# Nineteen joined score activations instead of thirteen, and one group of query transposes a place later, in a softcap attention with a soft mixture of experts on one core

## The chip, the cores and the metric

The kernel runs on one core of a Trainium2 chip. The metric is the device time of one execution in microseconds. The kernel before takes 281.36 us (median of three runs, 280.99 to 281.57).

Engine names are those of the profile: PE is TensorE (PEld its weight loads), ACT is ScalarE, DVE is VectorE, POOL is GpSimd, SP is SyncE. A line such as L366 is line 366 of the kernel.

## What is computed

Attention with a soft cap over 8 batches, 12 heads, 448 positions and 64 columns a head, then a soft mixture of eight experts over the 3584 rows of 768 columns that the attention leaves:

```python
scores = scale * np.matmul(q, k.transpose(0, 1, 3, 2))
scores = cap * np.tanh(scores / cap)
attn = np.exp(scores - max)                 # then divided by its sum
x = attn @ v                                # -> 3584 x 768
logits = x @ phi                            # 768 -> 32 slots
d = softmax(logits, over all rows)
slot_input = d.T @ x                        # 32 slots, 4 an expert
slot_out[e] = relu(slot_input[e] @ w1[e]) @ w2[e]
out = softmax(logits, over the slots) @ slot_out
```

## The kernel before, in words

**Tiles and steps.** Four heads of one batch are a *quad* (24 quads, three a batch); a quad has two pairs of heads, and a pair has seven *tiles*, each of 64 keys of both its heads against their 448 queries. That makes 336 tiles. `turn` puts them into one fixed order in which the second pair of a quad is interleaved with the first pair of the next one. The main loop (`for j in range(NCH)`) has 56 *steps* of six tiles. A step j has two *halves* of three tiles, i = 2j and 2j + 1.

**One step.** `qk_chunk(i)` computes the scores of a half: six matmuls on PE (L349) into three PSUM banks, a bank a tile. `tanh_chunk(i)` is the tanh on ACT, from PSUM to SBUF (L366, 128 x 1344 elements). `exp_chunk(j)` is the exponential on ACT, in SBUF (L374). Of most steps one, two or three of the six tiles are left out of it (`SHARED`), and DVE computes their exponential in seven instructions (`poly_exp`, L602 to L609), whose places in the loop are written out by hand in `POLY`. `pv_first`, `pv_tail` and `pv_rest` multiply the exponentials of a pair with its values on PE (L627), and `norm` ends the pair on DVE with a reciprocal (L634) and a multiplication (L637).

**Joined steps.** In the steps listed in `JOINED` one ACTIVATE (L362, 128 x 2688) does the tanh of both halves. From the first joined step to the last one the six score banks are one tile, the *board*, whose two halves are released separately; outside that stretch they are two tiles of three banks that take turns. In a joined step both halves come free together, at the end of that one ACTIVATE.

**The order of the work** is the order of the program: each engine takes its instructions in the order in which the loop emits them. A step has the slots 0, m, e, a, b, r, c and d, and each of them but r has a part ahead (`<`) and a part behind (`>`). In a step j: slot 0; the tanh of half 2j; slot m; the tanh of half 2j + 1 (in a joined step, here the one of both); slot e; the exponential of step j - 1; `pv_first`; slot a; `pv_tail`; `qk_chunk(2j + 2)` if the step isn't joined; slot b; `pv_rest` and `norm` (slot r between `norm`'s two instructions); `qk_chunk(2j + 2)` if the step is joined; slot c; `qk_chunk(2j + 3)`; slot d.

**The transposes.** `transp` turns the queries or the keys of a quad: 14 transposes on PE (L279) into one PSUM buffer (tag T, a single buffer, which the other transposes use too) and a copy on DVE to `qT` or `kT` (L281). `WHEN` gives the slots, counted from the batch's first step 7b. `k1` and `q1` are the keys and queries of quad 3b + 1; of batch 0 they have places of their own. From batch 1 on, `k1` stands in slot m and `q1` in slot b of step 7b. By the order of tiles, the first tile of quad 3b + 1 is the third tile of half 14b + 3, for every b from 1 to 7: that is `qk_chunk(2j + 3)` of the very same step j = 7b. Quads 3b + 1 have the numbers 4, 7, 10, 13, 16, 19 and 22; the steps 7b are 7, 14, 21, 28, 35, 42 and 49.

After the loop (L1053 and behind) come the end of the last batch, the two layers of the experts and the output.

Of the kernel before, what the change touches and what calls it, by code (L numbers as in the profile page):

```python
# [37 lines left out]
def kernel(  # L38
# [272 lines left out]
    def half_of(i):  # L311

        nonlocal psS
        j, half = divmod(i, CH // CS)
        if JOINED and half == 0 and j in (JOINED[0], JOINED[-1] + 1):
            scp.close()
            psS = scp.enter_context(tc.tile_pool(name=f"psS{j}", bufs=2 - (j == JOINED[0]), space=PSUM,
                                                 reuse_waits="tile"))
            if j == JOINED[0]:
                own["board"] = psS.tile([P, CH, 512], F32, name="sc", tag="board")  # L320
        if JOINED and JOINED[0] <= j <= JOINED[-1]:
            return own["board"][:, half * CS:half * CS + CS, :]
        return psS.tile([P, CS, 512], F32, name="sc", tag="sc")

    def in_board(j):
        return JOINED and JOINED[0] <= j <= JOINED[-1]

# [27 lines left out]
    def tanh_chunk(i):  # L355
# [3 lines left out]
        sc = scores.pop(i)  # L359
        if j in JOINED:  # L360
            if half:
# [16 lines left out]

    JOINED = (10, 14, 17, 21, 24, 28, 29, 31, 35, 38, 42, 45, 49)
    SHARED = {1: (2, 0), 3: (3, 0), 4: (3, 0), 6: (2, 0), 7: (3, 0), 9: (3, 0), 11: (3, 0), 12: (3, 0), 14: (3, 0), 16: (3, 0), 18: (3, 0), 19: (3, 0), 21: (3, 0), 23: (3, 0), 25: (3, 0), 26: (3, 0), 28: (3, 0), 30: (3, 0), 32: (3, 0), 33: (3, 0), 35: (3, 0), 37: (3, 0), 39: (3, 0), 40: (3, 0), 42: (3, 0), 44: (3, 0), 46: (3, 0), 47: (2, 0), 48: (2, 0), 49: (3, 0), 51: (2, 0), 52: (1, 0), 53: (3, 0), 54: (1, 0)}
    POLY = {(1, 'm'): ((1, 0),),
            (1, 'e'): ((1, 1),),
# [416 lines left out]
    def quad_in(Q, cast_k, cast_q, k_in, q_in, v_in):  # L801
        if 0 < Q < NQ:
# [5 lines left out]
                for n in range(2):  # L808
                    at(*v_in, vcast, Q, n)

    WHEN = {'k1': (0, 'm'), 'q1': (0, 'b'), 'v1': (3, 'c'), 'k2': (2, 'a'), 'q2': (2, 'd'), 'v2': (7, 'b'),
# [4 lines left out]
    for b in range(B):  # L816
        j, p = b * PER, 6 * b

        def when(nm):
            return j + WHEN[nm][0], WHEN[nm][1]  # L820

# [352 lines left out]
    for n in range(B // 2 * NT):  # L1174
        bb, c = divmod(n, NT)
# [59 lines left out]
```

## Time and profile before

| what | value |
|---|---|
| time, median of three runs | 281.36 us (280.99 to 281.57) |
| span of the profiled execution, first to last instruction | 279.2 us |
| PE matmul, busy | 247.0 us (88%) |
| ACT, busy | 248.6 us (89%) |
| DVE, busy | 239.1 us (86%) |
| POOL, busy | 142.0 us (51%) |
| granted clock of PE, mean | 0.985 |
| main loop, by ACT's rows | about 6 to 235 us |

The profiled execution's time is known from its span alone; the difference of 2.2 us to the median of the runs lies ahead of its first and behind its last instruction, or between executions. A row of the timeline reads: start in us from the span's start, length in us, engine, line, operation, what it writes <- what it reads, shape, count of instructions that the row merges, and in brackets the idle time of the engine before it with what ended it.

### The profile page before, as it was taken

To read this page: it belongs to the slowest core of one execution; us is meant where nothing else is said; L and a number is where in the kernel's file an instruction comes from. 1 tells how busy PE (TensorE), PEld (TensorE's weight loads), DVE (VectorE), ACT (ScalarE), POOL (GpSimd) and SP (SyncE) were. 2 spreads that over 40 slices of the span, in tenths; PEclk is the share of its full clock that TensorE was granted. 3 is DMA by queue.
4 is the path that set the end of the run, shared out by engine and by line. 5 is a ranking of instruction groups with operands and counts; after the bars stand their busy time and mean duration, and the time that the engine had idled before them with its cause. 6 is when DMAs were issued, how large, how long until landed. Compare 5 with 4: busy or idle time off the path is not lost.

```text
span 279.2 us, 10421 instructions
## 1 busy us (share of the span) xinstructions
PE 247.0 (88%) x4560; PEld 166.6 (60%) x4560; DVE 239.1 (86%) x473; ACT 248.6 (89%) x195; POOL 142.0 (51%) x198
## 2 busy tenths in 40 slices
PE   8898989998999999989999999899999999998720
PEld 7555556756675766566756675657566678553300
DVE  3479999999999999999999999999999997347940
ACT  4999999999999999999999999999999998237720
POOL 8796548662957296728673758375743230200000
PEclk9999999999999999999999999999999999999995
DMA  6999999999999999999999999999999588979997
GB/s 197 277 193 202 219 219 234 229 221 219 224 225 220 219 229 226 225 217 229 223 226 212 213 219 231 218 210 215 231 217 215 117 279 293 367 290 383 434 424 312
DMA packets 57340, 68.08 MB, mean 244 GB/s; under 512 B 4048, under 2 KB 53840, under 8 KB 56784
## 3 DMA queue, kind: packets, MB, share of 16 engines
q0 software_dynamic: 42448, 35.31, 80.0%
q1 hardware_dynamic: 14704, 32.02, 32.6%
q8 instruction: 35, 0.57, 0.7%
q10 hardware_dynamic: 144, 0.10, 0.1%
q14 instruction: 9, 0.07, 0.1%
HBM read 91.72 MB, written 19.27 MB: 398 GB/s over the span
## 4 chain that ended last, share of the span: by engine, by line
ACT 38%; DVE 27%; PE 27%; issue 3%; POOL 1%; ACTq 0%; DVEq 0%
ACT ex L366 15%; ACT ex L374 15%; PE pv L627 8%; ACT ex L362 6%; DVE xq L637 4%; PE sc L349 3%; DVE xp L605 3%; DVE xp L607 3%; DVE ex L608 2%; DVE ex L602 2%; PE so_ps L1098 2%; PE hp L1070 2%; DVE xf L604 2%; DVE ex L609 2%; DVE xp L606 2%
## 5 line engine op out<-in xcount | busy, mean ns | idle before, releaser
L366 ACT ACTIVATE ex<-sc 128x1344 f16<-128x1344 f32 (+1 forms) x87 | 112.9, 1402 | 0.9 <-PE sc L349 0.9
L374 ACT ACTIVATE ex<-ex 128x1344 bf16<-128x1344 f16 (+5 forms) x58 | 110.7, 1916 | 0.1
L627 PE MATMUL pv<-vbd,ex 128*128 128x130 bf16 (+1 forms) x1610 | 94.0, 212 | 7.6 <-POOL vbd L289 3.4
L627 PEld LDWEIGHTS <-ex 128*128 128x128 bf16 (+1 forms) x1680 | 75.6, 101 | 34.9 <-issue 6.2
L289 POOL CAST vbd<-vraw 64x896 bf16<-64x896 f32 x46 | 47.3, 1028 | 57.3 <-PE pv L627 35.7
L349 PE MATMUL sc<-qT,kT 64*64 64x448 bf16 x672 | 66.0, 359 | 6.7 <-ACT ex L366 4.8
L362 ACT ACTIVATE ex<-sc 128x2688 f16<-128x2688 f32 x13 | 33.6, 2586 | 0.0
L349 PEld LDWEIGHTS <-kT 64*64 64x64 bf16 x672 | 22.1, 105 | 16.3 <-ACT ex L366 6.9
L637 DVE TENSOR_TENSOR xq<-pv,rec 128x448 bf16<-128x448 f32 x46 | 28.7, 625 | 1.6
L607 DVE TENSOR_TENSOR xp<-xp,xf 128x1344 f16<-128x1344 f16 (+2 forms) x34 | 27.1, 798 | 0.6
L608 DVE TENSOR_TENSOR ex<-ex,xp 128x1344 uint16<-128x1344 uint16 (+2 forms) x34 | 26.9, 791 | 0.2
L605 DVE TENSOR_TENSOR xp<-xf 128x1344 f16<-128x1344 uint16 (+2 forms) x34 | 26.8, 789 | 0.2
L116 POOL DMA_DIRECT2D w1b<-in_moe_w_dram x32 | 26.3, 825 | 0.0
L602 DVE TENSOR_SCALAR ex<-ex 128x1344 uint16<-128x1344 f16 (+2 forms) x34 | 17.0, 500 | 1.4 <-ACT ex L366 0.8
L606 DVE TENSOR_SCALAR xp<-xp 128x1344 f16<-128x1344 f16 (+2 forms) x34 | 17.2, 505 | 0.6
L281 DVE COPY kT<-kps 128x896 bf16<-128x896 bf16 x23 | 14.2, 617 | 4.0 <-PE kps L276 2.8
L297 POOL MEMSET vbd<- 64x1 bf16 x22 | 2.8, 129 | 28.6 <-PE pv L627 28.3
L604 DVE TENSOR_SCALAR xf<-ex 128x1344 uint16<-128x1344 uint16 (+2 forms) x34 | 16.7, 491 | 0.4
L185 POOL DMA_DIRECT2D qb<-in_q_dram x22 | 16.3, 740 | 1.2 <-PE qps L279 0.5
L609 DVE TENSOR_SCALAR ex<-ex 128x1344 uint16<-128x1344 uint16 (+2 forms) x34 | 16.4, 483 | 0.4
L120 POOL DMA_DIRECT2D w2d<-in_moe_w_dram x21 | 16.4, 816 | 0.0
L185 POOL DMA_DIRECT2D kb<-in_k_dram x22 | 16.3, 739 | 0.0
(124 smaller groups left out, 320.2 us busy)
## 6 DMA issues: line engine op xcount, KB each, us to landing
w1b<-in_moe_w_dram POOLq DMA_DIRECT2D x32, 384.0 KB, 10.2
vraw<-in_v_dram SPq DMA_DIRECT2D x44, 224.0 KB, 6.2
w2d<-in_moe_w_dram POOLq DMA_DIRECT2D x21, 384.0 KB, 9.9
w2t<-w2d SPq DMA_DIRECT2D x21, 384.0 KB, 6.2
qb<-in_q_dram POOLq DMA_DIRECT2D x22, 224.0 KB, 8.2
kb<-in_k_dram POOLq DMA_DIRECT2D x22, 224.0 KB, 8.1
w2b<-in_moe_w_dram POOLq DMA_DIRECT2D x11, 384.0 KB, 9.5
out_dram<-ob SPq DMA_DIRECT2D x2, 1536.0 KB, 7.7
```

What stands on the lines that cost most here:

```text
L116: pool.dma_start(out=w1b[e][:, js, fs], in_=w1r[:, e, js, fs])
L185: pool.dma_start(out=t, in_=quad_ap(nm, Q))
L289: pool.tensor_copy(vbds[Q % 2][r, :, :, c0:c0 + DH], raw[r])
L349: ins = pe.matmul(sc[cs, u, 0:S], qkT["k", Q][r, c, cs], qkT["q", Q][r, :, cs], start=True, stop=True).ins
L362: apart["t", i - 1] = apart["t", i] = act.activation(exs[j].bitcast(F16), own["board"][:, :, 0:S], ACT.Tanh, scale=qk_scale / cap).ins
L366: ins = act.activation(exs[j][:, half * CS + u0:half * CS + u1, :].bitcast(F16), (own[0] if i == u0 == 0 else sc)[:, u0:u1, 0:S], ACT.Tanh ...
L374: act.activation(exs[j][:, u0:u1, :], exs[j][:, u0:u1, :].bitcast(F16), ACT.Exp, scale=cap)
L605: lambda: dve.tensor_tensor(p, s, s.bitcast(F16), op=ALU.mult),
L607: lambda: dve.tensor_tensor(p, p, s, op=ALU.mult),
L608: lambda: dve.tensor_tensor(y, y, p, op=ALU.add),
L627: pe.matmul(out_, exs[j][r, u, q0:q0 + (HP if tail else P)], v_, start=(c == 0 and g == gs[0] < NF), stop=(c == NT - 1), skip_group_check= ...
L637: dve.tensor_tensor(xq[Q][:, h, s0:s1, :], pv[:, 0:s1 - s0, 0:DH], rec.to_broadcast([P, s1 - s0, DH]), op=ALU.mult)
```

## The change

Six steps are added to `JOINED` (8, 15, 22, 36, 43 and 50), so that the board reaches from step 8 to step 50 instead of from 10 to 49. Step 29 was joined already, so after the change every step 7b + 1 is. And `q1` moves from slot b to slot c of step 7b, in batches 1 to 7: behind `pv_rest` and `norm`, and in the six of these steps that are joined (14, 21, 28, 35, 42, 49) behind `qk_chunk(2j + 2)` too. Nothing else changes.

```diff
-    JOINED = (10, 14, 17, 21, 24, 28, 29, 31, 35, 38, 42, 45, 49)
+    JOINED = (8, 10, 14, 15, 17, 21, 22, 24, 28, 29, 31, 35, 36, 38, 42, 43, 45, 49, 50)
...
-    WHEN = {'k1': (0, 'm'), 'q1': (0, 'b'), 'v1': (3, 'c'), 'k2': (2, 'a'), 'q2': (2, 'd'), 'v2': (7, 'b'),
+    WHEN = {'k1': (0, 'm'), 'q1': (0, 'c'), 'v1': (3, 'c'), 'k2': (2, 'a'), 'q2': (2, 'd'), 'v2': (7, 'b'),
```

## The prediction

> **What bounds the kernel now.** I read the page first, then the busy time of one stretch of the main loop, then single engines in order of time around the steps that the change touches. The span and the row of the half tanhs, from the page:
>
> ```profile
> span 279.2 us, 10421 instructions
> ```
> ```profile
> L366 ACT ACTIVATE ex<-sc 128x1344 f16<-128x1344 f32 (+1 forms) x87 | 112.9, 1402 | 0.9 <-PE sc L349 0.9
> ```
>
> Busy us in one stretch, in the order PE, PEld, DVE, ACT, POOL:
>
> ```profile
> 100.00:120.00 20.00, 18.75 (x383) 12.87 (x377) 19.43 (x38) 20.00 (x15) 13.89 (x19) 1.00 1.23 225
> ```
>
> ACT is busy 20.00 of 20.00 us, and in the whole execution its half tanhs waited 0.9 us for scores. DVE (19.43) and PE (18.75) follow closely, but where ACT never stops, ACT sets the end of the loop: a microsecond taken from it there is gained, and one for which it waits is lost.
>
> **What one joined tanh saves.** ACT, in order of time, from step 13 to step 15:
>
> ```profile
> 58.21 2.57 ACT L366 ACTIVATE ex<-sc 128x1344 f16<-128x1344 f32 x2
> 60.55 1.44 ACT L374 ACTIVATE ex<-ex 128x1344 bf16<-128x1344 f16 x1
> 61.76 2.53 ACT L362 ACTIVATE ex<-sc 128x2688 f16<-128x2688 f32 x1
> 64.05 2.57 ACT L374 ACTIVATE ex<-ex 128x2688 bf16<-128x2688 f16 x1
> 66.39 2.60 ACT L366 ACTIVATE ex<-sc 128x1344 f16<-128x1344 f32 x2
> ```
>
> The lengths mislead: two halves at 1.4 us each against 2.5 would be 0.3 us saved. But 58.21 + 2.57 = 60.78 lies behind the next start, 60.55: instructions overlap. What counts is from start to start: 60.55 - 58.21 = 2.34 for a pair, 64.05 - 61.76 = 2.29 for a joined one. So a join saves **0.05 us**, and six save 0.3 us, 0.1% of the time.
>
> [...]
>
> **What one joined tanh asks for.** A half tanh at 7b + 1 starts on the scores of half 2j + 2 (j = 7b), and those of half 2j + 3 have 1.17 us longer. The joined one needs both at the start. Half 2j + 3 holds the first tile of quad 3b + 1, so its last two matmuls read the queries that `q1` turns in this same step. Step 21, PE and DVE:
>
> ```profile
> 93.58 0.23 PE L627 MATMUL pv<-vbd,ex 64*64 64x65 bf16 x4
> ...
> 93.97 0.62 DVE L281 COPY qT<-qps 128x896 bf16<-128x896 bf16 x1
> ...
> 94.64 0.38 PE L349 MATMUL sc<-qT,kT 64*64 64x448 bf16 x2 [0.26 <-DVE qT L281]
> ```
> ```profile
> 94.69 2.72 ACT L366 ACTIVATE ex<-sc 128x1344 f16<-128x1344 f32 x2
> ```
>
> Two matmuls wait for the copy of `qT`, which ends at 94.59, and start 0.05 later. They end at 95.02. A joined tanh would already be held to about 95.07, against 94.69. Now the change puts this copy later still.
>
> **The moved step** issues 14 transposes on PE and one copy on DVE, no DMA and nothing on POOL or SP. On PE it goes behind `pv_rest` and (in joined steps) the six matmuls of half 2j + 2. On DVE the copy goes behind both instructions of `norm`, which wait for `pv_rest`, and behind exponential steps that stand at `>b` or `<c`. Step 28 shows all lengths, since its successor 29 is joined already. DVE, then PE, then ACT:
>
> ```profile
> 121.16 0.51 DVE L602 TENSOR_SCALAR ex<-ex 128x1344 uint16<-128x1344 f16 x1 [0.20 <-ACT ex L362]
> 121.59 0.50 DVE L609 TENSOR_SCALAR ex<-ex 128x1344 uint16<-128x1344 uint16 x1
> 122.01 0.62 DVE L281 COPY qT<-qps 128x896 bf16<-128x896 bf16 x1
> 122.54 0.50 DVE L604 TENSOR_SCALAR xf<-ex 128x1344 uint16<-128x1344 uint16 x1
> 122.96 0.20 DVE L634 RECIPROCAL rec<-pv 128x7 f32<-128x7 f32 x1
> 123.19 0.62 DVE L637 TENSOR_TENSOR xq<-pv,rec 128x448 bf16<-128x448 f32 x1
> 123.73 0.85 DVE L605 TENSOR_TENSOR xp<-xf 128x1344 f16<-128x1344 uint16 x1
> ```
> ```profile
> 122.15 0.49 PE L627 MATMUL pv<-vbd,ex 128*128 128x130 bf16 x5 [0.31 <-DVE ex L609]
> 122.44 0.38 PE L349 MATMUL sc<-qT,kT 64*64 64x448 bf16 x2
> 122.48 0.23 PE L627 MATMUL pv<-vbd,ex 64*64 64x65 bf16 x4
> 122.55 0.73 PE L349 MATMUL sc<-qT,kT 64*64 64x448 bf16 x10
> ```
> ```profile
> 123.33 2.44 ACT L362 ACTIVATE ex<-sc 128x2688 f16<-128x2688 f32 x1
> ```
>
> Read it as a chain. ACT's joined tanh of step 28 ends; DVE's L602 waited for it, and L609 stands behind L602; the last of `pv_rest` waits for L609 (0.31 us) and ends at 122.71. All 12 score matmuls are done at 123.28, and tanh 29 starts 0.05 later. Today the copy (122.01) is out of the way before `norm`.
>
> After the change, from the end P of `pv_rest`: reciprocal at P + 0.06 (122.77); to the multiplication 0.23 (122.96 to 123.19); to the next start 0.54 (123.19 to 123.73), where now the copy stands; copy 0.62; 0.05 to PE; two matmuls 0.38; 0.05 to ACT. That is 0.06 + 1.87 = **P + 1.93**. PE's transposes fit in beside it: behind the six matmuls, from about 122.93 to 123.51, while the copy can't start before 123.54. So tanh 29 starts at 122.71 + 1.93 = 124.64 instead of 123.33: **1.31 us lost**.
>
> **The seven places.** *28, 14 and 42*: 14 and 42 have the same order (first the step on the new tanh, then L609 of the older chunk, on which `pv_rest` waits), so taking `q1` away from before `pv_rest` gives nothing back: 1.3 us each, 3.9 us. That 14 and 42 hang on ACT in the same way show their rows of L602:
>
> ```profile
> 64.32 0.51 DVE L602 TENSOR_SCALAR ex<-ex 128x1344 uint16<-128x1344 f16 x1
> ```
> ```profile
> 177.94 0.51 DVE L602 TENSOR_SCALAR ex<-ex 128x1344 uint16<-128x1344 f16 x1 [0.34 <-ACT ex L362]
> ```
>
> (tanh 14 ended at 61.76 + 2.53 = 64.29.) *21*: here DVE comes free for the reciprocal at 93.97 (where the copy starts today), `pv_rest` having ended at 93.81. 93.97 + 1.87 = 95.84, and with 2.44 for the joined tanh it ends at 98.28; today's pair ends at 94.69 + 2.72 = 97.41: 0.9 us. *35*: as 21, but an L605 (0.85 us, `<c` of step 35) also stands ahead of the copy: 0.9 + 0.9 = 1.8 us. *49*: as 21, but the exponential that covers the chain is shorter,
>
> ```profile
> 206.26 2.03 ACT L374 ACTIVATE ex<-ex 128x1792 bf16<-128x1792 f16 x1
> ```
>
> 1792 elements in 2.03 us against 2688 in 2.57 at step 14 (64.05), some 0.6 us less cover: 1.5 us.
>
> *7* is another case. The board now begins at step 8, and its first use asks for both old score tiles. Step 9, where it begins today, shows this: half 20 starts when the second tanh ends (41.64 + 2.50 = 44.14), not the first.
>
> ```profile
> 41.64 2.50 ACT L366 ACTIVATE ex<-sc 128x1344 f16<-128x1344 f32 x2
> ...
> 44.19 0.56 PE L349 MATMUL sc<-qT,kT 64*64 64x448 bf16 x6 [0.34 <-ACT ex L366]
> ```
>
> Step 7 today, PE and ACT:
>
> ```profile
> 35.49 0.56 PE L349 MATMUL sc<-qT,kT 64*64 64x448 bf16 x6 [0.30 <-ACT ex L366]
> 35.98 0.58 PE L279 MATMUL qps<-ident,qb 128*64 128x128 bf16 x14
> 36.50 0.83 PE L627 MATMUL pv<-vbd,ex 128*128 128x130 bf16 x11
> 37.13 0.38 PE L349 MATMUL sc<-qT,kT 64*64 64x448 bf16 x2
> 37.16 0.23 PE L627 MATMUL pv<-vbd,ex 64*64 64x65 bf16 x4
> ```
> ```profile
> 34.15 2.46 ACT L366 ACTIVATE ex<-sc 128x1344 f16<-128x1344 f32 x2
> 36.49 1.71 ACT L374 ACTIVATE ex<-ex 128x1792 bf16<-128x1792 f16 x1
> 38.08 2.48 ACT L366 ACTIVATE ex<-sc 128x1344 f16<-128x1344 f32 x2
> ```
>
> Half 16 then starts at 34.15 + 2.46 + 0.05 = 36.66; `pv_rest` 0.49 later (35.49 to 35.98), and its end 0.89 behind that (36.50 to 37.39): P = 38.04. Tanh 8 starts at 39.97 and ends at 42.41; today's pair ends at 40.56: 1.85 us.
>
> **The sum**: 3.9 + 0.9 + 1.8 + 1.5 + 1.85 = 9.95 us, the gain of the joins being inside, since ends are compared. Some comes back: where DVE has gained a lead while ACT waits, the places 21 and 35 can be 0.3 us shorter, and 35 another 0.35 where `pv_rest` runs 0.4 earlier without the transposes ahead of it. I take 9.7 us. The span is 2.2 us under the median of the runs, and I take this rest as it is: 281.4 + 9.7 = **291.1 us**. ACT can't win it back: its exponential and tanhs behind each place stand as close as before.
>
> **What the later stages do.** Behind the joined tanh comes a 128 x 1344 exponential (1.21 us from start to start: 60.55 to 61.76), in which half 2j + 4 must be computed; at 29 that holds today. No stall is counted there; if the cover fails, up to 0.4 us a place is added.
>
> **Rivals.**
> *A, only the gain remains* (faster or no change): if half 2j + 3 had its queries in time, because the copy isn't behind `norm` in effect, six joins would save 0.3 us and the time would be 281.1 us. It decides wherever the copy ends before tanh 7b + 1 could start. ACT being the fullest engine speaks for it; the wait at 94.64 speaks against it. [...] Chance 0.06.
> *B, most of the wait is hidden*: if DVE's lead lets `norm` end before the joined tanh of 7b does, the copy waits only for the transposes, which stand behind the first half's matmuls: 0.05 + 0.49 + 0.58 + 0.06 + 0.62 + 0.05 + 0.38 + 0.05 = 2.3 us behind the tanh's end, about what the 2.3 us exponential covers. Then little but step 7 and 49 costs: about 285 us. Against it: L609 behind an L602 that waits for that very tanh, at three places. Chance 0.07.
> *C, the delay spreads*: PE, held up in front of half 2j + 3, brings the next `pv_first` and `norm` late as well, and half 2j + 4 misses its exponential by the 0.4 us of above: 7 x 0.4 = 2.8 more, 293.9 us. Chance 0.09.
>
> **How the numbers follow.** The forecast has 0.78, and its own range is 289 to 293 (each place 0.3 us either way). The range for 8 in 10 reaches a bit towards B and C: **287.8 to 293.5**. A measurement of this kernel can tell about 0.2% from no change, 0.6 us. Of A's 0.06, half is faster by that much, half isn't: faster 0.03, same 0.03, slower 0.94.
>
> **What would show it.** Right: ACT gaps ahead of L362 at steps 8, 15, 22, 29, 36, 43 and 50, of 0.9 to 1.9 us each, ended by PE sc L349; those two last matmuls waiting for DVE qT L281; the copy directly behind L637 (at 35 behind an L605); half 16 waiting for the second tanh of step 7; no other new gap on ACT. Wrong: joined tanhs at 7b + 1 that start without a gap (A), or gaps only at 8 and 50 (B), or gaps also ahead of the tanhs of 7b + 2 (C).

## The result, and the profile after

The changed kernel takes **292.09 us** (median of five runs, 291.55 to 292.98) against 281.36 us before: a ratio of 1.0379, 95% interval 1.0352 to 1.0406. Forecast were 291.1 us in a range of 287.8 to 293.5. The profiled execution has a span of 290.1 us, 10.9 more than before. Of all executions of the kernels told of below one, of the run four_joins, took 1093.67 us, and no median or ratio counts it.

The page of the changed kernel, the three groups of ACT's main loop (busy us and mean ns, then the idle time ahead of them and what ended it):

```profile
span 290.1 us, 10408 instructions
...
L374 ACT ACTIVATE ex<-ex 128x1344 bf16<-128x1344 f16 (+5 forms) x58 | 104.5, 1809 | 0.1
...
L366 ACT ACTIVATE ex<-sc 128x1344 f16<-128x1344 f32 (+1 forms) x75 | 93.6, 1304 | 1.6 <-PE sc L349 1.5
...
L362 ACT ACTIVATE ex<-sc 128x2688 f16<-128x2688 f32 x19 | 46.3, 2439 | 9.4 <-PE sc L349 9.4
```

The joined tanhs (L362), which waited for nothing before, now wait 9.4 us for scores. The view of all waits says how often:

```profile
ACT ex L362 <- PE sc L349: 9.4, 7, 1.8
...
PE sc L349 <- DVE qT L281: 4.8, 8, 1.3
```

Seven waits, and the second line says for what PE itself waited there: the copy of `qT`, 4.8 us in eight waits instead of 0.8 in three. Between the seven places ACT runs without a gap as before. The first row is the stretch of before; it has other steps in it now. Those that stood there run 4.53 us later (second row), and with them DVE is as full as it was (19.26 us of 20 against 19.43):

```profile
100.00:120.00 20.00, 18.78 (x382) 13.50 (x378) 18.22 (x35) 20.00 (x15) 11.88 (x18) 1.00 1.18 208
104.53:124.53 20.00, 18.83 (x382) 12.89 (x377) 19.26 (x38) 20.00 (x15) 12.79 (x18) 1.00 1.19 211
```

Step 28 and the joined tanh behind it, DVE, PE and ACT in order of time:

```profile
126.19 0.51 DVE L609 TENSOR_SCALAR ex<-ex 128x1344 uint16<-128x1344 uint16 x1
126.61 0.51 DVE L604 TENSOR_SCALAR xf<-ex 128x1344 uint16<-128x1344 uint16 x1
127.38 0.21 DVE L634 RECIPROCAL rec<-pv 128x7 f32<-128x7 f32 x1 [0.26 <-PE pv L627]
127.62 0.62 DVE L637 TENSOR_TENSOR xq<-pv,rec 128x448 bf16<-128x448 f32 x1
128.25 0.62 DVE L281 COPY qT<-qps 128x896 bf16<-128x896 bf16 x1
```
```profile
127.08 0.23 PE L627 MATMUL pv<-vbd,ex 64*64 64x65 bf16 x4
127.15 0.54 PE L349 MATMUL sc<-qT,kT 64*64 64x448 bf16 x4
127.62 0.58 PE L279 MATMUL qps<-ident,qb 128*64 128x128 bf16 x14
128.14 0.38 PE L349 MATMUL sc<-qT,kT 64*64 64x448 bf16 x4
128.93 0.38 PE L349 MATMUL sc<-qT,kT 64*64 64x448 bf16 x2 [0.41 <-DVE qT L281]
```
```profile
123.17 2.48 ACT L362 ACTIVATE ex<-sc 128x2688 f16<-128x2688 f32 x1
125.46 2.53 ACT L374 ACTIVATE ex<-ex 128x2688 bf16<-128x2688 f16 x1
129.34 2.41 ACT L362 ACTIVATE ex<-sc 128x2688 f16<-128x2688 f32 x1 [1.35 <-PE sc L349]
```

The copy now stands behind the multiplication of `norm` (L637), the last two matmuls of half 59 wait for it, and tanh 29 starts 0.03 us behind their end. The step's loss is read from ends: tanh 28 ends at 125.65 against 121.14 before (4.51 late), tanh 29 at 131.75 against 125.77 (5.98 late). So this place adds 1.46 to 1.47 us.

At step 7, half 16 waits for the second tanh, which ends at 37.19, and the joined tanh of step 8 for PE:

```profile
37.24 0.57 PE L349 MATMUL sc<-qT,kT 64*64 64x448 bf16 x6 [1.48 <-ACT ex L366]
```
```profile
40.56 2.41 ACT L362 ACTIVATE ex<-sc 128x2688 f16<-128x2688 f32 x1 [1.79 <-PE sc L349]
```

Done for every step, this gives nearly the whole difference. "Loss" is by how much the end of a step's last tanh falls further behind that of the kernel before; steps that aren't listed lose less than 0.05 us.

| step | forecast, us | loss, us |
|---|---|---|
| 8 | 1.85 | 1.84 |
| 15 | 1.3 | 1.32 |
| 22 | 0.9 | 0.83 |
| 29 | 1.3 | 1.46 |
| 36 | 1.8 | 1.63 |
| 37 | 0 | 0.21 |
| 43 | 1.3 | 1.32 |
| 50 | 1.5 | 1.39 |
| the seven places | 9.95 | 9.79 |

The rest of the 10.9 us is the start, where the first tanh comes 0.55 us later (among the other kernels here from 0.25 earlier to 0.70 later, with the same program up to there), and the part behind the loop, 0.4 us.

### The profile page after: what moved, and what is told of

Its sections match the earlier page's. It is cut to its first block, busy times and chain, and to the rows that moved or that the text cites. A ratio compares the mean times of both kernels' runs of the same rounds, so it can differ in the third digit from the quotient of the medians.

```text
span 290.1 us, 10408 instructions
## 1 busy us (share of the span) xinstructions
PE 252.3 (87%) x4560; PEld 167.6 (58%) x4560; DVE 240.6 (83%) x473; ACT 249.0 (86%) x189; POOL 141.1 (49%) x198
## 4 chain that ended last, share of the span: by engine, by line
DVE 36%; PE 33%; ACT 22%; issue 5%; ACTq 0%; DVEq 0%
PE pv L627 10%; ACT ex L366 9%; ACT ex L374 7%; PE sc L349 6%; DVE xq L637 5%; ACT ex L362 5%; DVE xp L605 4%; DVE ex L608 3%; DVE xp L607 3%; DVE ex L602 3%; DVE qT L281 3%; DVE xf L604 3%; DVE ex L609 3%; DVE xp L606 2%; PE so_ps L1098 2%
## 5 line engine op out<-in xcount | busy, mean ns | idle before, releaser
L374 ACT ACTIVATE ex<-ex 128x1344 bf16<-128x1344 f16 (+5 forms) x58 | 104.5, 1809 | 0.1
L366 ACT ACTIVATE ex<-sc 128x1344 f16<-128x1344 f32 (+1 forms) x75 | 93.6, 1304 | 1.6 <-PE sc L349 1.5
L627 PEld LDWEIGHTS <-ex 128*128 128x128 bf16 (+1 forms) x1680 | 76.4, 102 | 32.1 <-issue 7.8
L349 PE MATMUL sc<-qT,kT 64*64 64x448 bf16 x672 | 68.3, 362 | 14.3 <-ACT ex L366 5.8
L289 POOL CAST vbd<-vraw 64x896 bf16<-64x896 f32 x46 | 48.0, 1043 | 61.7 <-PE pv L627 42.9
L362 ACT ACTIVATE ex<-sc 128x2688 f16<-128x2688 f32 x19 | 46.3, 2439 | 9.4 <-PE sc L349 9.4
L637 DVE TENSOR_TENSOR xq<-pv,rec 128x448 bf16<-128x448 f32 x46 | 28.7, 625 | 1.6
L608 DVE TENSOR_TENSOR ex<-ex,xp 128x1344 uint16<-128x1344 uint16 (+2 forms) x34 | 27.3, 804 | 0.2
L605 DVE TENSOR_TENSOR xp<-xf 128x1344 f16<-128x1344 uint16 (+2 forms) x34 | 26.9, 790 | 0.2
L116 POOL DMA_DIRECT2D w1b<-in_moe_w_dram x32 | 25.6, 802 | 0.0
L689 DVE COPY xT<-xps 128x896 bf16<-128x896 bf16 (+1 forms) x24 | 14.3, 598 | 5.7 <-PE xps L680 5.7
L602 DVE TENSOR_SCALAR ex<-ex 128x1344 uint16<-128x1344 f16 (+2 forms) x34 | 16.9, 496 | 1.2 <-ACT ex L366 1.0
L604 DVE TENSOR_SCALAR xf<-ex 128x1344 uint16<-128x1344 uint16 (+2 forms) x34 | 17.0, 500 | 0.4
L609 DVE TENSOR_SCALAR ex<-ex 128x1344 uint16<-128x1344 uint16 (+2 forms) x34 | 16.5, 487 | 0.4
```

The costliest lines, as they stand in the source:

```text
L289: pool.tensor_copy(vbds[Q % 2][r, :, :, c0:c0 + DH], raw[r])
L349: ins = pe.matmul(sc[cs, u, 0:S], qkT["k", Q][r, c, cs], qkT["q", Q][r, :, cs], start=True, stop=True).ins
L362: apart["t", i - 1] = apart["t", i] = act.activation(exs[j].bitcast(F16), own["board"][:, :, 0:S], ACT.Tanh, scale=qk_scale / cap).ins
L366: ins = act.activation(exs[j][:, half * CS + u0:half * CS + u1, :].bitcast(F16), (own[0] if i == u0 == 0 else sc)[:, u0:u1, 0:S], ACT.Tanh ...
L374: act.activation(exs[j][:, u0:u1, :], exs[j][:, u0:u1, :].bitcast(F16), ACT.Exp, scale=cap)
L604: lambda: dve.tensor_scalar(s, y, STEP - 1, STEP, ALU.bitwise_and, ALU.bitwise_or),
```

## The experiments

The theory is the chain of the prediction: the end of the value products, reciprocal, multiplication, copy of `qT`, last two matmuls, joined tanh. The main rivals are that one part of the change costs by itself, the move or the joins. The losses by step in single profiles, in us; the first column is the changed kernel, the others stand in the order of the sections below, whose headings name them. The last five kernels of the table ran once each; for them the losses by step carry the argument, and not the time:

| step | changed | move_only | joins_only | inner_joins | step35_order | swap | q_in_norm | board_from_8 |
|---|---|---|---|---|---|---|---|---|
| 8 | 1.84 | 0 | 0.85 | 0 | 1.84 | 2.05 | 1.56 | 0.72 |
| 9 | 0 | 0 | 0.26 | 0 | 0 | 0.70 | 0 | 0 |
| 15 | 1.32 | 0.20 | 0.10 | 1.31 | 1.32 | 0.86 | 0.94 | 1.32 |
| 22 | 0.83 | 0 | 0.06 | 0.83 | 0.84 | 0.84 | 0.36 | 0.83 |
| 29 | 1.46 | 1.38 | 0 | 1.38 | 1.54 | 0.94 | 1.00 | 1.38 |
| 34 | 0 | 0 | 0 | 0 | 0 | 0 | 0 | 0.76 |
| 36 | 1.63 | 0.63 | -0.06 | 1.64 | 1.21 | 2.03 | 0.39 | 2.09 |
| 37 | 0.21 | 1.29 | 0 | 0 | 0 | 0 | 0 | 0.34 |
| 43 | 1.32 | 0.20 | 0.10 | 1.32 | 1.32 | 0.69 | 0.94 | 1.32 |
| 50 | 1.39 | 0.59 | 1.04 | 0.27 | 1.38 | 1.39 | 0.69 | 1.39 |

Not in the table are 0.36 us at step 46 in joins_only, 0.16 at 39 in move_only, 0.06 at 3 and 0.23 at 6 in swap, and 0.08 at 27 in step35_order.

### Only the move (move_only)

```diff
-    JOINED = (8, 10, 14, 15, 17, 21, 22, 24, 28, 29, 31, 35, 36, 38, 42, 43, 45, 49, 50)
+    JOINED = (10, 14, 17, 21, 24, 28, 29, 31, 35, 38, 42, 45, 49)
```

> The old thirteen joined steps, q1 in slot c. By the chain of the prediction (copy of qT behind norm, then two matmuls, then tanh), only a tanh 7b + 1 that needs both halves at its start pays in full, and that is step 29 alone: 1.4 us there. The other six start their second half 1.17 us later than a joined one would: 0.1 us at 15, 0 at 22, 0.5 at 36, 0.1 at 43, 0.2 at 50, and 0 at 8, where the board doesn't begin yet. Sum 2.3 us: about 283.7 us. By the rival that the move costs by itself, whatever is joined, at each of the seven places nearly what the whole change cost: above 289 us.

Measured: 286.42 us, ratio 1.0175 (1.0138 to 1.0212). Step 29, joined before, pays in full (1.38), and the other six pay 0 to 0.63: five of them within 0.13 us of the numbers expected, step 50 with 0.59 instead of 0.2. The total is 2.7 us above the expectation. 1.29 of that stand at one step where nothing was expected, 37, and the timeline of ACT shows a wait there:

```profile
157.94 1.28 ACT L366 ACTIVATE ex<-sc 128x1344 f16<-128x1344 f32 x1
160.41 1.29 ACT L366 ACTIVATE ex<-sc 128x1344 f16<-128x1344 f32 x1 [1.18 <-PE sc L349]
```

Busy time and clock of the same stretch (behind the five engines' busy times stands the granted clock of PE):

```profile
154.00:156.00 2.00, 0.87 (x16) 0.67 (x16) 1.27 (x4) 1.48 (x2) 1.17 (x2) 1.00 1.03 135
156.00:157.00 1.00, 1.00 (x22) 0.73 (x20) 0.96 (x3) 1.00 (x2) 0.00 (x0) 0.61 1.14 231
157.00:158.00 1.00, 1.00 (x10) 0.37 (x5) 0.28 (x1) 1.00 (x2) 0.00 (x0) 0.50 1.25 246
158.00:159.00 1.00, 1.00 (x14) 0.76 (x11) 0.00 (x0) 1.00 (x2) 0.08 (x1) 0.50 1.25 192
```

Behind a wait of 1.27 us PE ran at half its clock. No theory had that in its account; it comes back below.

### Only the joins (joins_only)

```diff
-    JOINED = (10, 14, 17, 21, 24, 28, 29, 31, 35, 38, 42, 45, 49)
+    JOINED = (8, 10, 14, 15, 17, 21, 22, 24, 28, 29, 31, 35, 36, 38, 42, 43, 45, 49, 50)
```

> All nineteen joined, q1 left in slot b. By the chain: a joined tanh waits for the last two matmuls where they end today, 0.1 us lost at 15, 22 and 43, 0 at 29 and 36, about 0.6 at 50, about 0.9 at 8 (where the board begins). Sum 1.8 us: about 283.2 us. With the run that only moves q1 that is 4.1 us, against 10.7 for both together: more than half of the loss belongs to neither part alone. By the rival that the joins cost by themselves (both halves come free at once, PE fills them too late): above 289 us.

Measured: 283.39 us, ratio 1.0074 (1.0041 to 1.0106), in the total near the 283.2 expected, but not place by place: 50 loses 1.04 instead of 0.6, steps 9 and 46, where nothing was expected, lose 0.26 and 0.36, and the loop of this execution began 0.23 us earlier. Neither part alone is the loss: 2.2 us for the joins and 5.2 for the move (both medians against 281.18), of which 1.3 stand at step 37; together with each other 10.7. More than half of that was expected to belong to neither part alone. By the medians it is 3.3 us, and at the seven places, where the move loses 3.0, the joins 2.1 and both together 9.8, it is 4.7, a little under half. At steps 15, 22 and 43 each part costs 0 to 0.2 us and both together 0.8 to 1.3. A tanh that starts on its first half hides the late second half, and an early copy of `qT` serves a joined one; the change takes away both.

### The joins at 8 and 50 left out (inner_joins)

```diff
-    JOINED = (8, 10, 14, 15, 17, 21, 22, 24, 28, 29, 31, 35, 36, 38, 42, 43, 45, 49, 50)
+    JOINED = (10, 14, 15, 17, 21, 22, 24, 28, 29, 31, 35, 36, 38, 42, 43, 45, 49)
```

> The changed kernel without the joins at 8 and 50, so that the board reaches from 10 to 49 as before. By the chain: nothing at step 8 (1.84 us less than the changed kernel), 0.2 us at 50 (1.2 less), the other five as in the changed kernel (1.32, 0.83, 1.46, 1.63, 1.32). Sum 6.8 us on ACT: about 288.9 us. By the rival that places feed each other (a loss early makes later ones smaller or larger): the five differ from those numbers by over 0.2 us.

Measured: 288.84 us in one run. Step 8 loses nothing, 50 loses 0.27, and the five others lose what they lost, within 0.08. By these five the places don't feed each other.

### One DVE instruction behind the copy (step35_order)

```diff
-            (35, '<c'): ((35, 2),),
+            (35, '>c'): ((35, 2),),
```

> The changed kernel with one DVE instruction of step 35, the L605 of 0.85 us, behind the copy of qT instead of ahead of it. By the chain: the loss at step 36 falls from 1.63 by about 0.75 to 0.9 us, to what step 22 loses (0.83), and all other places stay: 291.2 us. By the rival that DVE's order doesn't matter there because the transposes end last: no change, 292.1 us.

Measured: 291.64 us in one run, a time within those of the changed kernel. Step 36 loses 1.21 instead of 1.63; expected was about 0.83. The chain says why it isn't less. DVE in this run:

```profile
157.41 0.20 DVE L634 RECIPROCAL rec<-pv 128x7 f32<-128x7 f32 x1
157.64 0.62 DVE L637 TENSOR_TENSOR xq<-pv,rec 128x448 bf16<-128x448 f32 x1
158.18 0.61 DVE L281 COPY qT<-qps 128x896 bf16<-128x896 bf16 x1
158.71 0.85 DVE L605 TENSOR_TENSOR xp<-xf 128x1344 f16<-128x1344 uint16 x1
```

From the reciprocal's start to the tanh's (159.26) are 1.85 us, against 2.62 in the changed kernel (156.76 to 159.38), where L605 stood ahead of the copy: 0.77 us for the 0.85 of L605, as expected. But the reciprocal itself came later against the end of tanh 35: 1.64 us behind it (155.77) instead of 1.29 (155.47). How far DVE is behind at step 35 differs from run to run, and with it this place, 1.21 to 2.09 in the table.

### L609 ahead of L602 (swap)

```diff
-            (14, '<a'): ((14, 0), (12, 6), (14, 1)),
+            (14, '<a'): ((12, 6), (14, 0), (14, 1)),
...
-            (28, 'e'): ((26, 5), (28, 0)),
-            (28, '<a'): ((26, 6),),
+            (28, 'e'): ((26, 5), (26, 6)),
+            (28, '<a'): ((28, 0),),
...
-            (42, '<a'): ((42, 0),),
-            (42, '>a'): ((40, 6), (42, 1)),
+            (42, '<a'): ((40, 6),),
+            (42, '>a'): ((42, 0), (42, 1)),
```

> The changed kernel, with two neighbouring DVE instructions exchanged in steps 14, 28 and 42: L609 of the older chunk, on which the end of the batch of value products waits, now stands ahead of L602, which waits for that step's tanh. By the chain, the reciprocal then comes behind L602 and L604 at about 0.9 us after the tanh's end instead of 1.65, and the losses at steps 15, 29 and 43 fall from 1.32, 1.46 and 1.32 to between 0.5 and 0.85 us; the other places stay. About 290.2 us. By the rival that the transposes and PE's order set these losses, not DVE's queue: no change, 292.1 us.

Measured: 290.89 us in one run. Steps 15, 29 and 43 lose 0.86, 0.94 and 0.69 instead of 1.32, 1.46 and 1.32. The same instructions on PE and ACT, two neighbours exchanged on DVE, and 0.46 to 0.63 us less at each of the three places; of the other four none loses less: DVE's queue sets the end of the value products there. At step 28 they end 1.04 us behind the tanh's end (126.63 against 125.59) instead of 1.65. Of the three losses 0.69 lies within the 0.5 to 0.85 expected, 0.86 and 0.94 a little above. The time says less: steps 8 and 9 lost 0.9 us more in this run, with PE at half its clock from 38.36 to 45.19 us, step 36 lost 0.4 more, and the loop began 0.8 us earlier than in the changed kernel's profile.

### The copy between the two instructions of `norm` (q_in_norm)

```diff
-    WHEN = {'k1': (0, 'm'), 'q1': (0, 'c'),
+    WHEN = {'k1': (0, 'm'), 'q1': (0, 'r'),
```

> The changed kernel with q1 in slot r: PE turns the queries behind the value products but ahead of half 2j + 2, and DVE copies them between the two instructions of norm. By the chain the copy then waits for the transposes instead of the multiplication, and starts 0.6 us after the end P of the value products instead of 0.83; tanh 7b + 1 starts about 0.3 us earlier at six places, and at 36 about 1.1 us earlier, since L605 no longer stands ahead of the copy. Sum 2.9 us less: about 289.2 us. By the rival that the whole multiplication of norm is what is paid (PE's own order free): 0.55 us at six places and 1.4 at 36, about 287.4 us.

Measured: 287.75 us in one run. The gain is 0.28 to 0.47 us at five places, 0.70 at 50, 1.24 at 36. Step 28 again, DVE and PE:

```profile
126.17 0.20 DVE L634 RECIPROCAL rec<-pv 128x7 f32<-128x7 f32 x1 [0.26 <-PE pv L627]
126.65 0.62 DVE L281 COPY qT<-qps 128x896 bf16<-128x896 bf16 x1 [0.28 <-PE qps L279]
```
```profile
126.03 0.58 PE L279 MATMUL qps<-ident,qb 128*64 128x128 bf16 x14
126.54 1.17 PE L349 MATMUL sc<-qT,kT 64*64 64x448 bf16 x12
```

As the chain says, the copy now waits for the transposes (0.28 us). The matmuls no longer wait for the copy: 0.58 us of transposes and 12 matmuls in a row on PE set the start of the tanh, so the rival's condition, that PE's own order is free, doesn't hold. The tanh of step 29 starts 1.65 us behind P (126.10 to 127.75) instead of 2.03. The total, though, lies nearer to the rival's 287.4 than to the chain's 289.2: the places gain 3.9 us where the chain had 2.9, most of the surplus at 50 (0.70 instead of 0.3), where the copy starts 0.12 us behind the reciprocal's start (213.46 to 213.58) and no longer waits for the transposes, which end at 213.42. The 0.21 us of step 37 are gone too.

### The board from step 8, without the join there (board_from_8)

```diff
+    ONCE = tuple(j for j in JOINED if j != 8)
-        if j in JOINED:
+        if j in ONCE:
...
-        if j not in JOINED:
+        if j not in ONCE:
```

> The changed kernel with step 8 not joined, while the board of six banks still begins at 8 (so half 16 still waits for both tanhs of step 7). By the chain the second tanh of step 8 waits for half 17 at P + 1.93, 0.7 us lost there, against 1.84 joined and 0.00 in the run that only moved q1: so of the 1.84, 0.7 is the board's early start and 1.1 the join. About 291.0 us. By the rival that the early board alone makes the loss of step 8: 1.8 us stay.

Measured: 0.72 us at step 8, so the split is as expected: 0.7 for the board, 1.1 for the join. The time of this one run, 292.05 us, shows nothing of it: it also lost 0.76 at step 34, 0.46 more at 36 and 0.34 at 37, where the changed kernel had lost 0, 1.63 and 0.21. Ahead of step 34's second tanh PE stands still for 1.06 us, to 146.76, and the profile shows nothing that ended this; its cause stays open.

### Four joins with the transposes earlier (early_swap)

```diff
-    JOINED = (8, 10, 14, 15, 17, 21, 22, 24, 28, 29, 31, 35, 36, 38, 42, 43, 45, 49, 50)
+    JOINED = (10, 14, 15, 17, 21, 22, 24, 28, 29, 31, 35, 36, 38, 42, 43, 45, 49)
...
-    WHEN = {'k1': (0, 'm'), 'q1': (0, 'c'),
+    WHEN = {'k1': (-1, 'd'), 'q1': (0, 'a'),
```

with the exchange of L609 and L602.

> Joined at 15, 22, 36 and 43 beside the old thirteen (not at 8 and 50), with the keys' transposes a place earlier (end of the step before), the queries' in slot a, and L609 ahead of L602 at 14, 28 and 42. By the chain every joined tanh then finds its scores: no loss at 15, 22, 29, 36 and 43, four times 0.06 us gained, 281.1 us, within 0.2% of the kernel before. By the rival that a joined tanh right behind a joined one can't be fed whatever the order: 0.1 us or more lost at each place, 281.9 us or above.

A miss: 285.68 us, ratio 1.0157 (1.0136 to 1.0178). The joined tanhs at 15, 29, 36 and 43 are nearly fed (losses 0.17, 0, 0.11, -0.06), but new losses stand elsewhere: 1.24 at step 9, 0.95 at 22, 0.94 at 23, 0.53 at 37, 0.36 at 44. Step 7, DVE, POOL, and PE in the same stretch:

```profile
37.12 0.61 DVE L607 TENSOR_TENSOR xp<-xp,xf 128x896 f16<-128x896 f16 x1
37.77 1.36 DVE L608 TENSOR_TENSOR ex<-ex,xp 128x896 uint16<-128x896 uint16 x1
39.05 0.19 DVE L634 RECIPROCAL rec<-pv 128x7 f32<-128x7 f32 x1
```
```profile
37.72 0.92 POOL L289 CAST vbd<-vraw 64x896 bf16<-64x896 f32 x1 [3.80 <-PE pv L627]
```
```profile
40.05 1.07 PE L627 MATMUL pv<-vbd,ex 128*128 128x130 bf16 x14 [2.08 <-DVE xq L637]
```

L608 takes 1.36 us (0.63 at the same place in the kernel before) while POOL's cast runs; `norm` stands behind it, PE waits 2.08 us for `norm`, and from 40.73 us on it has half its clock. Moving a step on DVE had brought another instruction beside the cast. At step 22 the two copies, which wait for their transposes (0.46 and 0.58 us), now stand ahead of L609, and PE waits 1.34 us for L609; from 98.75 to 102.17 us, at step 23, PE has half its clock. Ahead of steps 37 and 44 an L604 of 1.24 us stands beside a cast (155.64 and 184.36 us).

### Four joins, q1 where it was, L609 ahead of L602 (inner_b_swap, and its two halves swap_alone and four_joins)

```diff
-    JOINED = (10, 14, 17, 21, 24, 28, 29, 31, 35, 38, 42, 45, 49)
+    JOINED = (10, 14, 15, 17, 21, 22, 24, 28, 29, 31, 35, 36, 38, 42, 43, 45, 49)
```

and the exchange as above.

> The kernel before (q1 in slot b) with four more joined steps (15, 22, 36, 43; the board from 10 to 49 as before) and L609 ahead of L602 in steps 14, 28 and 42. By the chain the joined tanhs at 15, 29 and 43 find their scores without a wait, 22 and 36 lose at most 0.06 us; a join gains 0.06 us, so about 0.2 us in all: 281.1 us, within 0.2% of before. By the rival that an exchange on DVE, whose queue is almost full, costs what it gives elsewhere: 0.5 us or more slower.

Measured: 282.52 us, ratio 1.0042 (1.0022 to 1.0062): 0.4% slower, where the same within 0.2% was expected. Losses: 0.12 at 15, 0.06 at 22, 0.23 at 36, 0.35 at 46, 0.42 at 50. Two further kernels take it apart.

> The kernel before with one edit: L609 ahead of L602 in steps 14, 28 and 42; no join and no transpose is moved. ACT hardly waits in the kernel before, so by the theory that ACT's own rows set the loop there is nothing to gain or to lose: 281.1 us, the same within 0.2%. By the rival that the exchange brings DVE's L604 beside POOL's cast (where it took 1.2 instead of 0.5 us in the run with both edits): 0.5 us or more slower, and then the joins aren't what cost in that run.

The exchange alone: 281.55 us, ratio 0.9999 (0.9976 to 1.0022). Nothing gained or lost.

> The kernel before with one edit: steps 15, 22, 36 and 43 joined too; q1 stays in slot b and the board from 10 to 49. By the places of the run with all the joins: 0.10 at 15, 0.06 at 22, -0.06 at 36, 0.10 at 43 and 0.36 at 46, no more: 0.5 us slower, about 281.7 us. By the rival that only the early board (8) and the late one (50) cost, and these four are free: 281.0 us.

The four joins alone: 282.21 us, ratio 1.0022 (1.0000 to 1.0044), with 0.10 at 15, 0.07 at 22, -0.06 at 36, 0.09 at 43, 0.03 at 46 and 0.45 at 50. The interval begins at no change, so that the joins cost little, if anything, with q1 early; what the profile shows of it stands for the most part at a step that wasn't touched, 50. ACT there in this kernel:

```profile
206.99 1.72 ACT L374 ACTIVATE ex<-ex 128x1792 bf16<-128x1792 f16 x1
209.04 2.47 ACT L366 ACTIVATE ex<-sc 128x1344 f16<-128x1344 f32 x2 [0.34 <-PE sc L349]
```

and in the kernel before:

```profile
206.26 2.03 ACT L374 ACTIVATE ex<-ex 128x1792 bf16<-128x1792 f16 x1
208.18 2.48 ACT L366 ACTIVATE ex<-sc 128x1344 f16<-128x1344 f32 x2
```

From start to start 2.05 and 1.92 us, though such an exponential takes 1.59 without a wait (36.49 to 38.08). The wait was there before as well, but hidden: the exponential of before ends at 208.29, behind the next start, that of this kernel at 208.71, 0.33 us ahead of it. The last section says more of this lead.

### PE kept busy in its waits (pe_kept_busy)

```diff
-    at(34, "<b", fill, 7)
+    at(34, "<b", fill, 7); at(7, "a", fill, 35); at(35, "c", spare, 6)
```

> The changed kernel with work without use for PE in its two longest waits: 35 small matmuls (1.2 us) ahead of half 16 in step 7, where PE waits 1.5 us, and two wide ones (0.5 us) behind the transposes of step 35, where it waits 1.27 us. In the changed kernel's profile PE's granted clock is 0.5 for 3.4 us behind the wait of step 35, and the executions with a lower mean clock take longer. If the waits are what lets the clock fall, no stretch of 0.5 is left in the loop, the mean clock of every execution is 0.984 or above, the 0.2 us at step 37 go and the seven places stay: about 291.4 us. If the falls have nothing to do with the waits: mean clocks from 0.970 to 0.985 as in the changed kernel, and 292.1 us.

Measured: 292.33 us (291.84 to 293.27), ratio 1.0391 (1.0365 to 1.0418): no gain. Its profile has no stretch of half clock in the loop and nothing lost at 37, but the same is so in profiles without this edit (inner_joins, step35_order, q_in_norm). The seven places lose 9.80 us. The mean clocks of its executions are 0.979 to 0.985, so that expectation failed; the mean also takes in the end of an execution, where the clock is lower (in the changed kernel's profile 0.50 from 282.78 us on), and says little of the loop. Nor do the changed kernel's five executions come in the order of their mean clocks: the one at 0.970 took longest (292.98 us) and the one at 0.985 least (291.55), but the one at 0.979 took 292.09 and one at 0.981 took 292.66. What the half clock costs the median stays open; in the profiles told of above with half clock there, step 37 loses 0.21 to 1.29 us.

## Why the prediction was right

**The bound.** ACT without a gap (busy 20.00 us of 20) sets the loop: right. What it waited for is what the execution grew by, place by place.

**0.05 us a join.** Right in size: where a joined tanh found its scores in time, at 36 without the move, it ended 0.06 us earlier than the pair. By the lengths it would have been 0.3 us.

**The chain to the joined tanh.** Right, by P + 2.03 instead of P + 1.93 at step 28 (127.31 to 129.34). The 0.1 us is the sentence "PE's transposes fit in beside it": they end at 128.21, and the copy starts at 128.25 instead of 128.16, 0.54 behind the multiplication's start. P itself comes 1.66 us behind the end of tanh 28 instead of 1.57, and these two make the 1.46 us out of the 1.28 that the chain gives by ends. At 14 and 42 the transposes end last as well. That the forecast 1.3 met 1.32 there is in part luck: before the change tanh 15 and 43 ended 4.69 us behind the tanh ahead of them, not 4.63 as at 29, so that by ends the chain gives 1.22 there, and the 0.1 us of the transposes makes up for it. The exchange of L609 and L602, the copy inside `norm` and L605 behind the copy each moved one link, and the losses followed.

**The seven places.** 9.79 us against a sum of 9.95 and 9.7 taken. Largest errors: 0.17 us at 36, which the runs with L605 ahead of the copy spread over 1.63 to 2.09, and 0.16 at 29. The board's part at step 8 was measured by itself (0.72 of 1.84).

**Step 7b + 2.** That half 2j + 4 keeps its cover was right (0.00 at every such step but 37). So rival C didn't come, nor did A or B. What did come at 37, and six times as much in the run of the move alone, stands at one of C's places but by a cause that no rival had, PE's clock: with half the clock, behind a wait of 1.27 us, 31 matmuls with the values take 2.74 us (from 159.47 us), while in inner_joins, behind the same wait but with the full clock, 35 take 1.92 (from 157.42 us) and step 37 loses nothing. These 0.21 us, the 0.55 at the start and the 0.4 behind the loop are what the profile has beyond the places.

**Where the sum was blind.** It priced the whole and not the parts. The parts' expectations were good for the joins (283.2 against 283.39), too low for the move (283.7 against 286.42), and wrong for the two versions that were to be as fast as the kernel before (281.1 expected; 285.68 for early_swap, 282.52 for inner_b_swap).

## What to carry to other kernels

Price a merge of instructions from start to start, not by their lengths, and set beside it what the merged instruction must have at its start: here 0.06 us of gain stood against 1.2 us of cover. Before moving a step, look for the first reader of what it makes; a reader in the same step can turn every instruction that it is moved past into latency. Two edits can cost little each (here 0 to 0.2 us at steps 15, 22 and 43) and much together (0.8 to 1.3), when each is the other's cover.

## What the runs showed of the hardware

**PE's clock fell behind some waits of 1.3 to 2.1 us, and not behind others.** In the changed kernel, busy time and clock in three stretches of 3.41 us:

```profile
156.49:159.90 3.41, 2.14 (x42) 1.28 (x36) 2.65 (x7) 1.83 (x2) 2.39 (x3) 1.00 1.19 168
159.90:163.32 3.42, 3.42 (x41) 2.25 (x39) 2.02 (x4) 3.32 (x3) 1.11 (x3) 0.50 1.19 212
163.32:166.73 3.41, 3.41 (x70) 2.29 (x70) 2.80 (x5) 3.41 (x3) 2.08 (x3) 1.00 1.06 156
```

The clock is 0.50 for 3.42 us and then back. Five profiles have such stretches in the loop, six in all, 3.41 to 3.42 us long, one of them twice that (swap, 38.36 to 45.19 us). Behind the loop the clock is 0.50 again, in the kernel before from 271.00 us and in the changed kernel from 282.78 us to the end. From the changed kernel's fall in the loop to this one are 282.78 - 159.90 = 122.88 us, 36 times 3.413; from the first fall to the second in early_swap (40.73 and 98.75 us) 58.02 us, 17 times as much. In the 3.41 us ahead of each of the six falls PE is busy 0.39 to 0.63 of the time, with a longest wait of 1.27 to 2.08 us. But stretches as long and no busier have no fall behind them: in early_swap one from 184.09 us with 0.48, and in joins_only the first of the two below. It is like the second, of swap, in PE's busy time (1.93 us) and longest wait (1.48 us), yet the clock fell behind the second alone:

```profile
34.64:38.05 3.41, 1.93 (x40) 1.27 (x37) 2.51 (x6) 3.34 (x3) 0.00 (x0) 1.00 1.22 233
```
```profile
34.95:38.36 3.41, 1.93 (x43) 1.31 (x43) 2.16 (x6) 3.29 (x3) 0.13 (x1) 1.00 1.22 233
```

So neither PE's busy share nor its longest wait tells by itself whether the clock falls. In the kernel before no stretch of 3.41 us between 100 and 230 us, wherever it is laid, has less than 0.70, and its clock never fell in the loop. In the changed kernel the clock fell behind the wait of 1.27 us at step 35 (to 158.97 us), but stayed at 1.00 behind the one of 1.48 us at step 7 (to 37.24 us). That waits cause the falls is argued from these profiles; the run with PE kept busy didn't show it by its time, and what decides stays open.

**A start ahead of the last end hid a wait.** Through the loop of the kernel before, ACT's half tanhs start every 1.17 us while their ends come every 1.18, so the lengths grow. Around step 29, in that kernel:

```profile
118.41 2.73 ACT L362 ACTIVATE ex<-sc 128x2688 f16<-128x2688 f32 x1
120.70 2.77 ACT L374 ACTIVATE ex<-ex 128x2688 bf16<-128x2688 f16 x1
123.33 2.44 ACT L362 ACTIVATE ex<-sc 128x2688 f16<-128x2688 f32 x1
```

At step 29 the joined tanh starts 2.63 us behind the exponential ahead of it (120.70 to 123.33) instead of 2.33, yet ends 2.30 behind that one's end (123.47 to 125.77), as every joined tanh without a wait does. A wait of 0.3 us in the starts cost nothing there. Once a larger wait has used the lead up, as at 50 in the run of the four joins (0.45 us lost), the same wait counted.

**DVE beside POOL's cast.** In the run of four joins with the exchange, DVE and POOL:

```profile
187.79 1.17 DVE L604 TENSOR_SCALAR xf<-ex 128x1344 uint16<-128x1344 uint16 x1
```
```profile
187.67 0.93 POOL L289 CAST vbd<-vraw 64x896 bf16<-64x896 f32 x1 [0.67 <-PE pv L627]
```

L604 mostly takes 0.50 us, and at the longest 0.60 in the kernel before. In seven places of the profiles told of here it takes 1.16 to 1.27 us, and all seven look like this one: the cast had begun 0.03 to 0.14 us ahead of it, ran its 0.93 us, and L604 ended 0.36 to 0.37 us behind the cast's end (here 188.96 and 188.60). Where a cast began 0.7 to 0.8 us ahead, so that only its last 0.2 us met L604, L604 took 0.56 or 0.57 and again ended 0.36 to 0.38 behind it. Where L604 began first, it kept 0.49 to 0.51 us, and the cast took up to 1.27 (longer the more of it the two overlapped). So in these profiles they hardly run side by side: the one that has begun finishes, and the other is stretched. The 0.35 us lost at step 46 stand behind this place, in this run and in joins_only (0.36 there), whose L604 is stretched at 188.31 us; without the stretch, in four_joins, the step loses 0.03. At another of the seven places (122.44 us, in swap_alone) the stretch cost ACT nothing. So on a full DVE (19.43 us of 20) the price of an exchange can be what it is brought beside.
